# Splitting weight conversion and weight-block preparation into two streams in a fused attention and two-layer feed-forward kernel

## The chip, the cores and the metric

The kernel runs on one core of one Trainium2 chip. The metric is the device time of one execution in microseconds (us). Three runs of the kernel before gave 1201.35, 1202.36 and 1206.76 us; their median, 1202.36 us, is what the change is compared with.

## The reference

Attention with RMS-normalised queries and keys, then two feed-forward layers over the same 1792 tokens.

```python
q, k, v: (4 batches, 12 heads, 448 tokens, 64)
attn = softmax(rmsnorm(q, g_q) @ rmsnorm(k, g_k).T / 8)      # with max subtraction
x = (attn @ v), heads joined: (1792, 768)
h = relu(x @ w_in)                     # w_in  768 x 2048
y = (h * h) @ w_out                    # w_out 2048 x 768
g = y @ w_gate;  val = y @ w_val       # 768 x 1536 each
out = (g * sigmoid(g) * val) @ w_out2  # w_out2 1536 x 768, out (1792, 768)
```

## The kernel before

All results are float32. A feed-forward product is computed with each operand cut in a high part (a cast to the multiplier's format) and a low part (what the cast left over), as high by high, high by low and low by high: three matmuls for one. Against that, the blocks are combined in a seven-product scheme (Strassen's), so that a 2 by 2 block of products takes seven groups P1 to P7 instead of eight. The inputs of the groups are sums and differences of blocks of weights (A11, A12, A21, A22) and of activations (B11, B21, B22, T1 to T4).

**Stages.** Attention comes first. Then for each layer (ph is 0 or 1): an up stage, in which a *quad* (two 128-column slabs of the up weights) yields seven groups of 9 matmuls for each of two token halves (tp is 0 or 1), 14 groups in all; and a down stage of 7 x ng steps of 18 matmuls (ng is 8 in the first layer, 6 in the second), in the order P2, P5, P3, P1, P6, P7, P4. The first up stage has 8 quads, the second 12.

**Weights.** They arrive as 64-bit words, 768 KB a slab, in one of two *raw regions* (L245). Four instructions convert a slab to float32 in one of five buffers called conv: a ScalarE cast (L282) and on VectorE one tensor_scalar (L283) and two scalar_tensor_tensor (L256). A *block* is then a high cast on ScalarE (L458) and a low subtraction on VectorE (L259) into one of the five slots of the ring. The even slabs of the down weights are converted straight into the area dn during the down stage (area jobs); the odd ones during the up stage, sent to DRAM (wkeep, L331) and brought back (L339).

**Up results.** Groups are evicted from PSUM (ps) by ScalarE or VectorE into 448-column slots of xacc, taken from a list called free. Each finished block, and the sums T1, T2 and T4 (GpSimd) and T3 (VectorE), is sent to DRAM (hid, L960). A down step n fetches its pair of blocks (448 KB, L1153), casts it (L1166) and subtracts for the low part (L997) into one of three buffers; this splitting is called cleave, and step n does it for step n + 2.

**What sets the order.** Every engine runs its own instructions in the order in which the program issues them. One generator, stream, yields conversions, sums, casts and low parts in a fixed sequence. pump, called once in each step, takes instructions from it until a budget of VectorE time is spent or the next one's gate is closed; need takes them regardless until the block that TensorE wants is there. A raw slab may be converted three counts of clock after its load was issued (the clock counts groups, two for a down step). All DMAs of this part are issued by SyncE's queue (SP), which waits in order too.

## Time and profile before

| | |
|---|---|
| time, median of 3 runs | 1202.36 us |
| the profiled execution's own time | 1212.9 us |
| its span, first to last instruction | 1211.1 us |
| TensorE (PE) busy | 1151.8 us, 95% |
| VectorE (DVE) busy | 893.8 us, 74% |
| ScalarE (ACT) busy | 627.6 us, 52% |
| GpSimd (POOL) busy | 328.7 us, 27% |
| chain that ended last | PE 69%, DVE 13%, DMA 7%, ACT 6% |
| DMA moved | 183.30 MB, mean 151 GB/s |

The profiled execution took 10.5 us more than the median run. A PE that is called busy need not be at its peak: the granted clock fell in parts of the span, and a matmul takes longer there. The shares are averages over attention (to about 251.7 us), the first up stage (to 472.2 us), the first down stage (to 719 us), the second up stage (to 1031.5 us) and the second down stage; the rows further down are by stage.

### The profile page before, as it was taken

How to read it: one execution, taken by the hardware profiler on the slowest of the kernel's cores; microseconds unless marked ns; L12 is line 12 of the kernel's file. 1: busy time of each engine (PE TensorE's matmuls, PEld its weight loads, DVE VectorE, ACT ScalarE, POOL GpSimd, SP SyncE). 2: the span in 40 equal slices, each digit the busy share in tenths (PEclk: the TensorE clock that was granted, in tenths of full speed). 3: DMA queues.
4: the chain of work that ended last, by engine and by line, in shares of the span. 5: the costliest groups of instructions: out<-in, count | busy, mean ns of one | idle time of the engine just before them, and what ended most of it. 6: DMA issues, size and time to landing. Idle time of an engine off the chain costs nothing.

```text
span 1211.1 us, 17115 instructions
## 1 busy us (share of the span) xinstructions
PE 1151.8 (95%) x6164; PEld 960.0 (79%) x6164; DVE 893.8 (74%) x1185; ACT 627.6 (52%) x1031; POOL 328.7 (27%) x304
## 2 busy tenths in 40 slices
PE   8999999999998998778999999999999999789998
PEld 5555555579887886667999999999999999678997
DVE  7777888678887887567766787868678595776553
ACT  6777886668454555343544445444343433445332
POOL 5899999621422334000000000202112020200000
PEclk9999999999999998888999999999999999899999
DMA  6444331114766768943543400635244453944554
GB/s 172 113 117 127 94 100 56 40 33 134 268 233 206 225 210 303 322 147 113 167 144 122 122 31 25 209 126 193 98 152 141 136 198 106 332 144 122 167 168 136
DMA packets 112997, 183.30 MB, mean 151 GB/s; under 512 B 13329, under 2 KB 94993, under 8 KB 112913
## 3 DMA queue, kind: packets, MB, share of 16 engines
q1 hardware_dynamic: 112592, 182.22, 46.6%
q8 instruction: 48, 0.79, 0.3%
q14 instruction: 37, 0.30, 0.1%
q10 hardware_dynamic: 320, 0.00, 0.0%
HBM read 125.96 MB, written 56.05 MB: 150 GB/s over the span
## 4 chain that ended last, share of the span: by engine, by line
PE 69%; DVE 13%; DMA 7%; ACT 6%; issue 4%; SPq 1%; POOL 1%; ACTq 0%; DVEq 0%; POOLq 0%
PE ps L1035 29%; PE ps L1200 23%; PE s L707 5%; PE s L692 5%; DMA xacc<-in_moe_w_in_dram 2%; DVE conv L256 2%; ACT xacc L1000 2%; PE s L663 2%; DVE xacc L997 2%; DVE ring L259 2%; PE s L631 2%; PE s L728 2%; DMA dn<-hid 1%; DMA xacc<-in_moe_w_out_dram 1%; DVE conv L283 1%
## 5 line engine op out<-in xcount | busy, mean ns | idle before, releaser
L997 POOL TENSOR_TENSOR xacc<-xacc 128x448 f32<-128x448 f32 x84 | 116.2, 1406 | 648.4 <-DVE xacc L997 503.7
L1200 PE MATMUL ps<-xat,ring 128*128 128x448 f32 x1008 | 222.4, 383 | 24.6 <-ACT ring L458 12.7
L1200 PEld LDWEIGHTS ps<-xat,ring 128*128 128x128 f32 x1008 | 197.8, 197 | 49.3 <-ACT ring L458 14.9
L1035 PE MATMUL ps<-xb,ring 128*128 128x448 f32 x1080 | 228.7, 367 | 0.9 <-ACT xacc L1000 0.9
L1035 PEld LDWEIGHTS ps<-xb,ring 128*128 128x128 f32 x1080 | 202.7, 188 | 20.5 <-ACT xacc L1000 1.3
L1200 PE MATMUL ps<-xab,ring 128*128 128x448 f32 x756 | 162.6, 376 | 13.4 <-ACT ring L458 5.9
L1200 PEld LDWEIGHTS ps<-xab,ring 128*128 128x128 f32 x756 | 144.6, 193 | 31.2 <-ACT ring L458 7.3
L1035 PE MATMUL ps<-xat,ring 128*128 128x448 f32 x720 | 159.3, 370 | 5.3 <-DVE xacc L997 5.3
L1035 PEld LDWEIGHTS ps<-xat,ring 128*128 128x128 f32 x720 | 135.9, 189 | 19.6 <-DVE xacc L997 6.8
L259 DVE TENSOR_TENSOR ring<-conv,ring 128x384 fp32r<-128x384 f32 x118 | 83.8, 725 | 61.1 <-ACT ring L458 60.0
L1035 PE MATMUL ps<-xab,ring 128*128 128x448 f32 x540 | 119.4, 371 | 3.9 <-ACT ring L458 3.9
L1000 ACT ACTIVATE xacc<-ps 128x448 f32<-128x448 f32 x148 | 77.9, 547 | 78.6 <-PE ps L1035 62.5
L997 DVE TENSOR_TENSOR xacc<-ps,xacc 128x448 f32<-128x448 f32 x180 | 106.5, 615 | 15.6 <-PE ps L1035 9.7
L1035 PEld LDWEIGHTS ps<-xab,ring 128*128 128x128 f32 x540 | 102.3, 190 | 15.0 <-ACT ring L458 4.3
L256 DVE SCALAR_TENSOR_TENSOR conv<-xacc,conv 128x768 int32<-128x768 int32 x108 | 111.3, 1031 | 3.4
L666 DVE TENSOR_REDUCE mxz<-s 112x2 f32<-112x896 f32 x96 | 100.4, 1088 | 16.5 <-PE s L663 16.3
L458 ACT CAST ring<-dn 128x384 fp32r<-128x384 f32 x82 | 41.7, 514 | 135.0 <-PE ps L1200 103.4
L698 POOL TENSOR_TENSOR sg<-p 112x896 f32<-112x896 f32 x46 | 96.9, 2107 | 14.2 <-ACT p L694 14.2
L458 ACT CAST ring<-conv 128x384 fp32r<-128x384 f32 x118 | 58.5, 510 | 79.4 <-DVE conv L256 34.0
L694 ACT ACTIVATE p<-s 112x896 f32<-112x896 f32 x96 | 87.8, 919 | 20.2 <-PE s L692 15.3
L1000 ACT ACTIVATE xacc<-xacc 128x448 f32<-128x448 f32 x132 | 74.6, 575 | 45.3 <-DVE xacc L997 43.5
L259 DVE TENSOR_TENSOR ring<-dn,ring 128x384 fp32r<-128x384 f32 x82 | 45.9, 566 | 54.7 <-ACT ring L458 54.5
(97 smaller groups left out, 1459.1 us busy)
## 6 DMA issues: line engine op xcount, KB each, us to landing
hid<-xacc SPq DMA_DIRECT2D x196, 224.0 KB
dn<-hid SPq DMA_DIRECT2D x98, 448.0 KB
xacc<-in_moe_w_out_dram SPq DMA_DIRECT2D x28, 768.0 KB
xacc<-in_moe_w_in_dram SPq DMA_DIRECT2D x16, 768.0 KB
xacc<-in_moe_w_gate_dram SPq DMA_DIRECT2D x12, 768.0 KB
xacc<-in_moe_w_val_dram SPq DMA_DIRECT2D x12, 768.0 KB
raw<-in_k_dram SPq DMA_DIRECT2D x24, 224.0 KB
raw<-in_q_dram SPq DMA_DIRECT2D x24, 224.0 KB
```

What stands on the lines that cost most here:

```text
L256: nc.vector.scalar_tensor_tensor(out=out, in0=in0, scalar=scalar, in1=out, op0=op, op1=ALU.bitwise_or)
L259: nc.vector.tensor_tensor(out=out, in0=a, in1=b, op=ALU.subtract)
L458: fn(*args)
L666: nc.vector.tensor_reduce(out=mxz[:, c, 0:P:D], in_=ps[:CP, :, :S], op=ALU.max, axis=AX.X)
L692: nc.tensor.matmul(ps[:CP, a, :S], lhs, rhs, start=(w == 0), stop=(w == 3))
L694: nc.scalar.activation(out=p, in_=ps[:CP, :, :S], func=AF.Exp)
L698: nc.gpsimd.tensor_tensor(out=sg, in0=p_t[pi, 2 * w], in1=p_t[pi, 2 * w + 1], op=ALU.add)
L707: nc.tensor.matmul(ps[s, :S], v_t[pi][:, a, c * D:(c + 1) * D], p[:, a, :], start=(c == 0), stop=(c == NCH - 1),)
L997: eng.tensor_tensor(out=o, in0=a, in1=b, op=op)
L1000: nc.scalar.activation(out=slot(s), in_=src, func=func)
L1035: nc.tensor.matmul(ps, w[:, wi, kk * P:(kk + 1) * P], xk[:, xi, kk * S:(kk + 1) * S], start=bool(first and mm == 0), stop=(mm == 3 * KT - ...
L1200: nc.tensor.matmul(ps_of(ps[tp, o]), w[:, wi, o * P:(o + 1) * P], h[:, hi, tp * S:(tp + 1) * S], start=bool(first and m == 0), stop=(g == ...
```

## The change

The one stream becomes two. convert_all (queue C) converts slabs in their order as soon as a slab has landed and a conv buffer is free; stream (queue B) makes sums and blocks, and waits by gates for what C has made. The low subtraction of a block is put in a third list (L), and is issued at the earliest in the call of pump after the one that issued its cast. pump goes through L, B, C in this order. Buffers are given back by name (spent, busy) instead of by position.

```diff
+    def convert_all():
+        for n, (ph, what, a, b, i) in enumerate(jobs):
+            if what == "area":
+                yield from area_job(ph, a, i)
...
+            c = convs[k % NCONV]
+            free_ = lambda k=k: k < NCONV or k - NCONV in spent
...
+                yield from convert(i, c, free_)
...
-    def block(entry, src, also=None):
+    def block(entry, src, key, gate=None, since=None, done=None):
         n = at[entry]
         r = ring[n % RING]
+        def low():
+            minus(r[:, 1], src, r[:, 0].bitcast(F32))
+            ready.add(n)
...
         yield act(nc.scalar.copy, r[:, 0], src,
-                  gate=lambda: state["used"] >= n - RING + 1 and (also is None or also()))
-        yield dve(0.55, minus, r[:, 1], src, r[:, 0].bitcast(F32))
-        ready.add(n)
+                  gate=lambda: state["used"] >= n - RING + 1 and (gate is None or gate()),
+                  soft=lambda: state["tick"] > (since() if t is None else t))
+        lows.append((state["tick"], n, low))
...
+    def emit(limit, spend, streams):
+        state["tick"] += 1
+        while True:
+            for s in streams:
+                if s == "L":
+                    if lows and lows[0][0] < state["tick"] and limit():
+                        lows.pop(0)[2]()
+                        spend(0.55)
+                        break
+                    continue
+                op = peek(s)
+                if can(op) and (op[0] == "act" or limit()):
+                    cost = run_op(s)
...
     def pump(budget):
-        state["debt"] = min(state["debt"] + budget, budget + 1.5)
+        state["debt"] = min(state["debt"] + budget, budget + 2.0)
...
+        emit(lambda: state["debt"] > 0, spend, "LBC")
```

A third raw region is laid over xacc slots 3 to 6 when these are free. It is claimed in the first up stage from quad 2 on (and again early in a down stage), and the free list has four slots fewer while it is. A load takes the region that was emptied first, and in the up stages a region is filled again three counts of clock after its conversion instead of two.

```diff
     def raw_of(i):
-        a = 16 * S + (b // 2) * 4 * S + (b % 2) * 2 * KH
+        a = (16, 20, 3)[region[i]] * S
...
+        lag = 3 if dn.get("ph") is None else 2
...
+            fit = [r for r in range(3) if valid(r) and (r not in last_in or old(r) + lag <= clock["n"])]
+            region[i] = r = min(fit, key=old)
```

The sums T1 to T4 are issued one count after their inputs instead of up to three, and a slot goes back to the free list when its last reader has been issued (drop). In the down stage the fetch of step n + 5 becomes that of step n + 4, a block from wkeep may be cast two counts after its bring instead of three, pump is called twice in a step with half the budget, and the low half of a cleave goes behind the second call. The first fetches of a down stage are issued in the P3 groups instead of after P7.

```diff
-            for new, needs in (("T1", {"B11": 3, "B12": 1}), ("T3", {"B22": 1, "T1": 1}), ("T2", {"B22": 2, "T1": 3}),
-                               ("T4", {"B21": 3, "T2": 3})):
+            for new, needs in (("T1", ("B11", "B12")), ("T3", ("B22", "T1")), ("T2", ("B22", "T1")), ("T4", ("B21", "T2"))):
...
-                    t = when[new] = max(when[x] + d for x, d in needs.items())
+                    t = when[new] = max(when[x] for x in needs) + 1
...
-                    bring(ph, 1)
-                    stage(ph, 0)
-                    bring(ph, 2)
-                    stage(ph, 1)
-                    bring(ph, 4)
-                    stage(ph, 2)
+                if q_ == last and p == "P3":
+                    bring(ph, 1 + 3 * tp)
+                    stage(ph, tp)
+                    bring(ph, 2 + 3 * tp)
+                    stage(ph, 1 + tp)
...
+                rate = 2.8 if n < 2 * ng else 2.3
+                pump(rate / 2)
                 cleave(n + 2, 0)
-                cleave(n + 2, 1)
                 run_due()
-                stage(ph, n + 5)
+                stage(ph, n + 4)
...
-                pump(2.9 if n < 2 * ng else 2.2)
+                pump(rate / 2)
+                cleave(n + 2, 1)
```

No engine has an instruction more or less than before; what changes is the order, and which buffer is used. Three places show it. The lines of the changed kernel have other numbers: L289, L261, L264 and L267 are what L283, L256, L259 and L262 were, L1014, L351, L360, L247 and L1217 what L960, L331, L339, L245 and L1153 were, and L1054 is L997.

The first place is DVE in the first up stage, around the end of one quad and the beginning of the next; rows with conv on both sides of an int32 operation are conversions, rows that write ring are low parts. Before:

```order
L259 TENSOR_TENSOR ring_85<-conv_77,ring_85 128x384
L283 TENSOR_SCALAR conv_79<-conv_79 128x768
L256 SCALAR_TENSOR_TENSOR conv_79<-xacc,conv_79 128x768 x2
L283 TENSOR_SCALAR conv_80<-conv_80 128x768
L256 SCALAR_TENSOR_TENSOR conv_80<-xacc,conv_80 128x768 x2
L997 TENSOR_TENSOR xacc<-ps,xacc 128x448
L283 TENSOR_SCALAR conv_76<-conv_76 128x768
L256 SCALAR_TENSOR_TENSOR conv_76<-xacc,conv_76 128x768 x2
L259 TENSOR_TENSOR ring_82<-conv_78,ring_82 128x384
```

Now:

```order
L264 TENSOR_TENSOR ring_85<-conv_76,ring_85 128x384
L289 TENSOR_SCALAR conv_76<-conv_76 128x768
L261 SCALAR_TENSOR_TENSOR conv_76<-xacc,conv_76 128x768 x2
L267 TENSOR_TENSOR ssum<-conv_76 128x384
L264 TENSOR_TENSOR conv_76<-conv_80,conv_76 128x384
L1054 TENSOR_TENSOR xacc<-ps,xacc 128x448
L264 TENSOR_TENSOR ring_82<-conv_77,ring_82 128x384
L264 TENSOR_TENSOR ring_86<-conv_80,ring_86 128x384
L289 TENSOR_SCALAR conv_77<-conv_77 128x768
L261 SCALAR_TENSOR_TENSOR conv_77<-xacc,conv_77 128x768 x2
```

The three conversions that stood together ahead of a block's low part are spread between low parts and sums.

The second place is SP at the end of the first up stage, where the results of the last quad are sent and the first pieces of the down stage (dn) are fetched. Before:

```order
L960 DMA hid<-xacc 128x448
L331 DMA wkeep<-conv_80 128x768
L245 DMA xacc<-in_moe_w_out_dram 128x1536
L960 DMA hid<-xacc 128x448 x3
L339 DMA dn<-wkeep 128x2x384
L1153 DMA dn<-hid 128x896
L339 DMA dn<-wkeep 128x2x384
L1153 DMA dn<-hid 128x896
L339 DMA dn<-wkeep 128x2x384 x2
L1153 DMA dn<-hid 128x896
```

Now:

```order
L351 DMA wkeep<-conv_79 128x768
L247 DMA xacc<-in_moe_w_out_dram 128x1536
L1014 DMA hid<-xacc 128x448 x15
L360 DMA dn<-wkeep 128x2x384
L1217 DMA dn<-hid 128x896
L360 DMA dn<-wkeep 128x2x384
L1217 DMA dn<-hid 128x896
L1014 DMA hid<-xacc 128x448
L360 DMA dn<-wkeep 128x2x384 x3
L1217 DMA dn<-hid 128x896
```

The last raw load and the last wkeep now stand fifteen sends ahead of the first fetch instead of three, and five wkeep pieces are fetched here instead of four.

The third place is DVE at the first two steps of the first down stage. Rows that write xat are low halves of a cleave, rows that write dn from xacc or dn convert an area slab. Before, from the cleaves of steps 1 and 2 on:

```order
L997 TENSOR_TENSOR xat<-dn,xat 128x896 x2
L997 TENSOR_TENSOR xacc<-xacc 128x448
L283 TENSOR_SCALAR dn<-dn 128x2x384
L256 SCALAR_TENSOR_TENSOR dn<-xacc,dn 128x2x384 x2
L259 TENSOR_TENSOR ring_84<-dn,ring_84 128x384
L283 TENSOR_SCALAR dn<-dn 128x2x384
L256 SCALAR_TENSOR_TENSOR dn<-xacc,dn 128x2x384
```

Now, from the low parts of the first two blocks on:

```order
L264 TENSOR_TENSOR ring_83<-dn,ring_83 128x384
L264 TENSOR_TENSOR ring_84<-dn,ring_84 128x384
L1054 TENSOR_TENSOR xat<-dn,xat 128x896
L264 TENSOR_TENSOR ring_85<-dn,ring_85 128x384
L264 TENSOR_TENSOR ring_86<-dn,ring_86 128x384
L264 TENSOR_TENSOR ring_82<-dn,ring_82 128x384
L289 TENSOR_SCALAR dn<-dn 128x2x384
L261 SCALAR_TENSOR_TENSOR dn<-xacc,dn 128x2x384 x2
L1054 TENSOR_TENSOR xacc<-xacc 128x448
L289 TENSOR_SCALAR dn<-dn 128x2x384
L261 SCALAR_TENSOR_TENSOR dn<-xacc,dn 128x2x384
L1054 TENSOR_TENSOR xat<-dn,xat 128x896
```

The blocks of the first five steps come ahead of the first conversion instead of the first block alone, and the cleave of step 2 comes behind one and a half conversions.

## Rows read from the trace of the kernel before

**Rows 1.** Windows: us; busy us and instructions of each engine; clock, DMA share, GB/s.

```profile
251.70:472.20 220.50, 210.34 (x1012) 191.11 (x1008) 183.27 (x233) 129.24 (x239) 64.40 (x47) 0.98 0.60 198
472.20:567.40 95.20, 70.59 (x289) 60.23 (x288) 59.02 (x83) 37.20 (x57) 7.31 (x6) 0.87 0.66 232
567.40:719.00 151.60, 151.60 (x720) 137.66 (x721) 110.88 (x143) 69.04 (x102) 0.00 (x0) 0.98 0.39 120
719.00:1031.50 312.50, 312.50 (x1514) 283.85 (x1513) 234.32 (x343) 133.23 (x238) 44.91 (x33) 1.00 0.41 136
1031.50:1110.70 79.20, 65.84 (x291) 56.88 (x289) 56.62 (x80) 33.95 (x54) 5.99 (x4) 0.94 0.57 197
1110.70:1207.50 96.80, 96.78 (x467) 87.58 (x467) 51.53 (x71) 36.04 (x55) 0.00 (x0) 1.00 0.50 158
```

**Rows 2.** Timeline, PE, first up stage: start, us, instruction, count, idle time before.

```profile
255.44 3.81 PE L1035 MATMUL ps<-xb,ring 128*128 128x448 f32 x18
259.09 3.81 PE L1035 MATMUL ps<-xat,ring 128*128 128x448 f32 x18
```

**Rows 3.** Timeline, one late slab in the first up stage, four engines.

```profile
375.40 0.76 SPq L245 DMA_DIRECT2D xacc<-in_moe_w_in_dram  x1
...
381.85 0.89 ACT L282 ACTIVATE conv<-xacc 128x768 f32<-128x768 f32 x1 [10.14 <-DMA xacc<-in_moe_w_in_dram]
...
382.77 0.56 DVE L283 TENSOR_SCALAR conv<-conv 128x768 int32<-128x768 int32 x1 [4.82 <-ACT conv L282]
...
385.91 3.73 PE L1035 MATMUL ps<-xab,ring 128*128 128x448 f32 x9 [3.90 <-ACT ring L458]
```

**Rows 4.** Timeline, from the first up stage to the first down stage.

```profile
468.45 0.59 SPq L339 DMA_DIRECT2D dn<-wkeep  x1
469.10 0.66 SPq L1153 DMA_DIRECT2D dn<-hid  x1
...
470.22 1.98 PE L1035 MATMUL ps<-xlast,ring 128*128 128x448 f32 x9
...
476.31 0.94 ACT L1166 CAST xat<-dn 128x896 fp32r<-128x896 f32 x1 [2.73 <-DMA dn<-hid]
...
477.72 0.74 PE L1200 MATMUL ps<-xat,ring 128*128 128x448 f32 x1 [5.51 <-ACT ring L458]
```

**Rows 5.** Timeline, from the second up stage to the second down stage.

```profile
1024.88 0.59 SPq L1153 DMA_DIRECT2D dn<-hid  x1
...
1027.96 0.77 SPq L1153 DMA_DIRECT2D dn<-hid  x1
...
1029.31 0.94 ACT L1166 CAST xab<-dn 128x896 fp32r<-128x896 f32 x1 [11.90 <-DMA dn<-hid]
...
1036.54 0.94 ACT L1166 CAST xab<-dn 128x896 fp32r<-128x896 f32 x1 [2.22 <-DMA dn<-hid]
```

**Rows 6.** Groups by line, DVE, 465 to 570 us: busy us, mean ns, idle before.

```profile
L997 DVE TENSOR_TENSOR xat<-dn,xat 128x896 fp32r<-128x896 f32 x18 | 19.8, 1100 | 21.6 <-ACT xat L1166 21.6
L256 DVE SCALAR_TENSOR_TENSOR dn<-xacc,dn 128x768 int32<-128x768 int32 x16 | 15.3, 957 | 0.5
L259 DVE TENSOR_TENSOR ring<-dn,ring 128x384 fp32r<-128x384 f32 x12 | 6.5, 552 | 2.0 <-ACT ring L458 2.0
...
L283 DVE TENSOR_SCALAR dn<-dn 128x768 int32<-128x768 int32 x8 | 4.4, 555 | 7.0 <-ACT dn L282 7.0
```

**Rows 7.** Timeline, DVE and POOL side by side, second down stage's first steps.

```profile
1029.53 7.97 POOL L997 TENSOR_TENSOR xacc<-xacc 128x448 f32<-128x448 f32 x5 [0.71 <-DVE xacc L997]
...
1031.56 1.48 DVE L259 TENSOR_TENSOR ring<-dn,ring 128x384 fp32r<-128x384 f32 x1
```

**Rows 8.** Windows, first down stage's first 30 us; the last figure is GB/s.

```profile
472.20:483.90 11.70, 5.78 (x19) 4.42 (x19) 5.70 (x8) 6.30 (x11) 7.31 (x6) 0.71 1.05 402
483.90:502.00 18.10, 13.63 (x56) 11.59 (x56) 12.47 (x17) 6.55 (x9) 0.00 (x0) 0.91 1.01 350
```

**Rows 9.** Chain of waits in order of time, near 304 us: start, us, what.

```profile
303.86 5.10 DMA hid<-xacc
```

More of the change, by code (lines that the diff above doesn't have):

```diff
@@ L69 @@
     clock = {"n": 0}
-    state = {"turn": 1, "used": 0, "debt": 0.0, "down": -1, "step": -1, "limit": 4}
+    state = {"turn": 1, "used": 0, "debt": 0.0, "down": -1, "step": -1, "limit": 4, "tick": 0, "third": False}
     def slot(s):
@@ L247, in load_raws, with waiting, dve, act @@
             nsent["n"] += 1
[L249 to L253 removed]
+    def waiting(rs):
+        return [i for i in sent if i not in turned and region[i] in rs]
+    def dve(cost, fn, *args, gate=None, soft=None):
+        return ("dve", cost, fn, args, gate, soft)
+    def act(fn, *args, gate=None, soft=None):
+        return ("act", 0.0, fn, args, gate, soft)
     def stt(out, in0, scalar, op):
@@ L441, in stream @@
-                if n % 3 != 2 and evens < ng:
-                    assert p == "P2" or evens > g
-                    evens += 1
-                    yield from conv_next(ph, "area", None)
-                if ph == 0 and p == "P1" and g % 2:
-                    yield from conv_next(1, "quad", carry)
-    steps = stream()
-    ahead = []
-    def peek():
-        if not ahead:
-            ahead.append(next(steps, None))
-        return ahead[0]
-    def run_op():
-        _, cost, fn, args, _ = ahead.pop()
+                    t, tk = spare.pop(0)
@@ L1133, in up @@
                         state["down"] = 100 * ph + level
+                if ph == 0 and q_ >= 2 and not state["third"] and len(free) >= 8 and all(s in free for s in (3, 4, 5, 6)):
+                    claim_third()
                 if q_ == last and tp == 1 and p == "P7":
@@ L1192, in down @@
                 if n == ng - 1:
+                    assert not due
                     free.clear()
+                if n < ng and not state["third"] and all(s in free for s in (3, 4, 5, 6)):
+                    claim_third()
+                if n == 2 * ng:
+                    state["third"] = False
+                if n == 3 * ng - 1:
+                    assert not waiting((2,))
                 first = g == 0 and p in ("P2", "P5", "P1")
```

321 lines of the change are left out of this document (175 added, 146 removed).

## The prediction

> **What bounds the kernel now.** I read the page first: TensorE is busy 95% of the span, so a time can only come out of the places where it isn't, or where its clock is low. The busy time by windows finds them [rows 1]. In the second up stage and in the late parts of both down stages PE has no idle time. In the other three windows it has, and its granted clock is 0.98, 0.87 and 0.94 there. The price of a stage without any loss comes from two neighbouring pieces of the timeline: 18 matmuls start 3.65 us after the 18 before them [rows 2], so a down step is 3.65 us, a group of nine 1.825. In the second half 467 matmuls take 96.8 us [rows 1], 3.73 us a step. From that the losses:
>
> First up stage: 8 quads of 14 groups are 112 groups, 204.4 us; it takes 220.5: 16.1 us lost. First down stage: the 720 matmuls of the third window leave 288 of 1008, 16 steps, 58.4 us; they take 95.2 (the gap ahead of them included): 36.8 lost. Second down stage: 756 - 467 = 289 matmuls, 16 steps, 59.9 us; they take 79.2: 19.3 lost. Together 72 us, and that is all that a new order of the same instructions can win.
>
> Then who ends PE's waits. In the up stage, once in most quads, a slab that is late: its load goes out at 375.40, ScalarE stands 10.14 us until it lands at 381.85, DVE converts from 382.77, and PE, which had waited 3.90 us, goes on at 385.91 at a lower clock [rows 3]. At the end of that stage SP issues the first fetch of the down stage at 468.45, the activations follow at 469.10 and are cast at 476.31, and PE has waited 5.51 us [rows 4]. In the down stage DVE is short of nothing but order: the low halves of 18 cleaves had 21.6 us of idle time ahead of them, spent waiting for the high casts, and the conversions 7.0 [rows 6]. DVE is busy only 59.0 of 95.2 us there [rows 1], while PE waits for it.
>
> **The change, part by part.** No engine gets or loses an instruction. What is won is waiting, and each stage has a new limit that decides how much.
>
> First down stage. P7 of the last quad ends three groups ahead of the last group's start, at 470.22 - 5.5 = 464.7 [rows 4]. Before, SP reaches the first fetch 3.7 us after that, because a late wkeep and a raw load stand just ahead of it; now fifteen sends lie between. With nothing in its way the fetch goes out at about 465, the activations 0.65 us behind it. In the second down stage, where SP is free, they need 1029.31 - 1024.88 = 4.4 us [rows 5], so they are there at 470.1, cast and subtracted (0.94 and 1.10 us) at 472.1, as PE finishes its last group. The 5.5 us go.
>
> Late next is step 2. Its fetch is the eighth of this burst instead of the seventh. The seventh was cast 1036.54 - 1024.88 = 11.7 us after the first [rows 5]; one more wkeep piece is 0.39 MB, 1.0 us at 402 GB/s [rows 8]. So it lands at 465.5 + 12.7 = 478.2, the fifth wkeep piece a microsecond earlier. DVE's piece of step 0 in the new order is three low parts, one sum, one and a half conversions and the cleave: 3 x 0.552 + 0.6 + 2 x 0.555 + 3 x 0.957 + 1.1 = 7.3 us [rows 6], from 477.1 to 484.4. Beside it POOL makes the last quad's sums. A low part that took 0.552 us took 1.48 beside those, five of which fill 7.97 us [rows 7]. The low parts here stand ahead of most of POOL's work, so I take two to three such lengthenings, 2.4 us; the bounds are none and, if all eight of its two-input instructions suffer, 7.4. Step 2 starts at 486.8 instead of 479.4.
>
> This is where a page speaks against the change. The Trainium skill ("SBUF — State Buffer", section "Who interferes with whom") says that a VectorE instruction with two SBUF inputs and a GpSimd instruction that reads SBUF exclude each other, the later one standing still for the whole of the other. By it DVE would lose up to the full 8 us of POOL's sums, 5.6 more in each down stage, and the forecast would be 11 us higher; the 0.93 us of the row is less than a POOL sum of 1.6, so the trace bears out the conflict and not the whole price.
>
> From there DVE sets the pace. In the new order steps 0 to 15 hold 16 cleave lows, 18 scalar_tensor_tensor, 9 tensor_scalar, 19 ring lows, 26 sums of that size and one 0.6: 17.6 + 17.2 + 5.0 + 24.8 + 0.6 = 65.2 us [rows 6] against 58.4 for PE. What is left after step 0, 57.9 us, ends at 544.7, when step 17 can start; with 3 us for gaps and slabs that land late, 548. Without loss it would start at 472.1 + 17 x 3.65 = 534.2. The loss is 14, with a microsecond for the clock 15 instead of 36.8: 22 us won. DMA hides behind this: by step 7 the new order has asked for about 14.4 MB since 465 (8 wkeep pieces of 0.39 MB, 9 fetches of 0.46, 5 raw slabs of 0.79, 14 sends of 0.23), 35.8 us at 402 GB/s or 41.1 at 350 [rows 8], so until 501 or 506, and DVE comes to the last of these slabs at about 510. If that cover is gone, the second rival below is the price. Bounds of this term: 10 (every step waits for DMA) to 29.
>
> Second down stage. It had no late SP, so its first step starts at 1031.5 as before. Step 2's activations come one wkeep piece later, 1037.5; DVE's first piece ends at 1036.4 + 7.3 + 2.4 = 1046.1, 7 us late. Steps 0 to 11 hold 12 x 1.1 + 12 x 0.957 + 6 x 0.555 + 38 x 0.552 + 0.6 = 49.6 us; the remaining 42.3 end at 1088.4, with 2 us for gaps 1090.4, and step 13 without loss would be at 1080.0. The loss is 10.4 instead of 19.3: 9 us won, bounds 3 and 14.
>
> First up stage. Raw loads go to three regions, and a slab is converted about a quad ahead of its use instead of three to five groups ahead, so the wait of rows 3 falls on engines and not on PE. But DVE needs 183.3 of 204.4 us [rows 1], and the new order puts the conversions of the whole stage into its first five sixths, where it leaves DVE nothing over. I take 7 us of loss instead of 16.1: 9 won. The row nearest is the busy time of DVE; bounds are 13 (only the first quads' tightness remains) and minus 4 (below nothing, by the waits of the third rival).
>
> The second up stage and attention have no loss to give; their orders shift by an instruction or two, and I cost them at nothing, since PE covers both (234 us of DVE in 312.5).
>
> Sum: 22 + 9 + 9 = 40 us. The profiled execution took 1212.9, so 1172.9; the median was 10.5 lower, which makes 1162.
>
> **Rivals.** *DMA takes the place of DVE.* A fetch is now issued two steps, 7.3 us, ahead of its cast, one step later than before. One at the head of the queue needs 4.4 us, one behind six others 8.6 [rows 5]. While raw slabs are loaded each may be 1.3 us late: 8 + 6 steps of P2 give 18 us back, and 40 - 18 = 22 leave 1180. For it: 402 and 350 GB/s right there [rows 8]. Against: a fetch that is late hits ScalarE first, and the cast has a further step in hand. The Trainium skill ("DMA: Bandwidth & Descriptors", "Where 436 GB/s comes from") gives some 358 GB/s as what HBM grants a core; 14.4 MB would then take 40.2 us, and this rival would be likelier; the 402 of the trace speak against so low a ceiling.
>
> *Slower: slots that are still being sent.* The third region takes four slots, so the free list holds six instead of ten in the up stage, and in each quad from the fourth on the evictions of P5 (both halves) and of P6's first go into slots whose send was issued one or two groups, 1.8 to 3.7 us, before. A send can take 5.10 us [rows 9]. Three waits of 3.3 are 9.9 us a quad; ScalarE is busy 129.2 us in 8 quads, 16.2 of 25.5, and has 9.4 to spare: so it decides from sends of about 5 us on. At 8.6 us, as long as a fetch in the burst, the waits are 20.4 and exceed it by 11 us in each of five quads: 55 lost, 31 won in the down stages, 24 slower, 1226. Against it: sums are issued earlier, SP's queue isn't tied to PE's steps, and DMA is busy only 0.60 of that stage.
>
> *No change.* The streams wait for each other through the five conv buffers and the same ring, the third region is rarely free, and what the low parts win is lost in the new bursts: 1200.
>
> **How the numbers follow.** The forecast has 0.61 (its own range 1146 to 1175), the DMA rival 0.24 (1175 to 1194), no change 0.06, slower 0.09. About 0.5%, 6 us, is what can be told from no change. Faster by more: 0.85; within: 0.06; slower: 0.09. The range that leaves out two in ten runs from 1142, the sum of the best bounds being 56 won and so 1146, less a little for the clock, to 1190.
>
> **What would show it.** Right, if PE's gap ahead of the first down stage is under 1.5 us, the first 16 steps there take 70 to 77 us instead of 95.2 with DVE busy over 85% of them, a gap of several us stands ahead of step 2 in both down stages, no low half of a cleave waits long for its cast, and the first up stage takes 208 to 215 us. Wrong, if ScalarE waits in the down stage mostly for DMA (first rival), if evictions in the up stage wait for hid sends and PE's gaps there grow (second), or if the second up stage, now without a gap, gets some.

## The result and the profile after

The changed kernel takes 1175.4 us (median of 4 runs, 1174.2 to 1177.2) where the kernel before takes 1203.9 (4 runs, 1201.4 to 1206.8): a ratio of 0.976, 95% interval 0.974 to 0.979. That is 28.5 us faster; 40 were forecast. The time lies inside the outer range of 1142 to 1190, and just beyond the forecast's own 1146 to 1175, on the border to the 1175 to 1194 of the DMA rival: the number alone does not decide between the two, the stages below do. The profiled execution took 1177.2 us, 35.7 less than the profiled one of before.

The windows of the changed kernel, cut at the same points of the program as [rows 1]: us; busy us and instructions of each engine; clock, DMA share, GB/s.

```profile
251.46:467.74 216.28, 211.31 (x1012) 191.17 (x1008) 182.08 (x236) 135.45 (x245) 69.83 (x49) 0.98 0.65 217
467.74:543.23 75.49, 64.83 (x288) 57.27 (x288) 64.84 (x94) 35.31 (x55) 4.76 (x4) 0.93 0.74 260
543.23:692.79 149.56, 147.16 (x720) 135.03 (x721) 103.78 (x132) 66.48 (x98) 0.00 (x0) 1.00 0.38 117
692.79:1006.56 313.77, 312.75 (x1514) 283.55 (x1512) 232.84 (x342) 133.50 (x240) 44.88 (x33) 1.00 0.41 136
1006.56:1076.10 69.54, 63.46 (x290) 56.40 (x290) 57.49 (x82) 33.12 (x54) 4.76 (x3) 0.95 0.64 222
1076.10:1171.80 95.70, 95.20 (x469) 87.57 (x467) 50.38 (x68) 36.15 (x56) 0.00 (x0) 1.00 0.50 160
```

Stage by stage against [rows 1]: first up stage 220.5 to 216.3, first 16 steps of the first down stage 95.2 to 75.5, the rest of it 151.6 to 149.6, second up stage 312.5 to 313.8, first 16 steps of the second down stage 79.2 to 69.5, the rest 96.8 to 95.7. Sum of the differences: 35.4 us, of which 29.4 in the two starts of down stages. (L1092 and L1271 are the matmuls that were L1035 and L1200, L490 and L1230 the casts of blocks and activations that were L458 and L1166; L1293 evicts.)

The step into the first down stage, PE and then DVE, which answer to [rows 4] and [rows 7]: start, us, instruction, count, idle time before and its releaser.

```profile
465.71 2.02 PE L1092 MATMUL ps<-xlast,ring 128*128 128x448 f32 x9
467.74 0.47 PE L1271 MATMUL ps<-xat,ring 128*128 128x448 f32 x1
468.75 0.47 PE L1271 MATMUL ps<-xat,ring 128*128 128x448 f32 x1 [0.54 <-DVE xat L1054]
471.63 9.01 PE L1271 MATMUL ps<-xat,ring 128*128 128x448 f32 x35 [2.41 <-DVE ring L264]
...
467.32 1.38 DVE L1054 TENSOR_TENSOR xat<-dn,xat 128x896 fp32r<-128x896 f32 x1 [0.21 <-ACT xat L1230]
468.62 1.55 DVE L1054 TENSOR_TENSOR xacc<-xacc 128x448 f32<-128x448 f32 x1
470.10 0.61 DVE L1054 TENSOR_TENSOR xacc<-ps,xacc 128x448 f32<-128x448 f32 x1
470.63 2.36 DVE L264 TENSOR_TENSOR ring<-dn,ring 128x384 fp32r<-128x384 f32 x2
```

The 5.5 us ahead of the stage are gone. What stands there now is 2.41 us at the third matmul, which waits for the low part of the first weight block (L264); DVE has a sum and an eviction ahead of it. Beside POOL's sums the times that these instructions take alone, 1.09, 0.62 and two of 0.55 us, have become 1.38, 1.55 and 2.36 (the two together): 2.5 us more in all, and the prediction had taken 2.4.

Next the queue of SyncE (SPq) and ScalarE a few steps on.

```profile
474.02 0.32 SPq L1217 DMA_DIRECT2D dn<-hid  x1
474.39 5.31 SPq L1014 DMA_DIRECT2D hid<-xacc  x6
480.89 0.32 SPq L1217 DMA_DIRECT2D dn<-hid  x1
481.26 0.52 SPq L360 DMA_DIRECT2D dn<-wkeep  x1
...
476.76 0.95 ACT L1230 CAST xat<-dn 128x896 fp32r<-128x896 f32 x1 [0.65 <-PE ps L1271]
485.43 0.51 ACT L490 CAST ring<-dn 128x384 fp32r<-128x384 f32 x1 [7.72 <-DMA dn<-wkeep]
485.84 0.94 ACT L1230 CAST xat<-dn 128x896 fp32r<-128x896 f32 x1
491.68 0.51 ACT L490 CAST ring<-dn 128x384 fp32r<-128x384 f32 x1 [4.90 <-DMA dn<-wkeep]
```

The fetch at 480.89 fills a staging buffer that DVE has only just emptied, and the wkeep piece stands behind it in the queue: asked for at 481.26, cast at 485.43, after ScalarE has stood for 7.72 us. PE's gaps of 1.74 and 2.76 us at 493.9 and 497.1 come behind the second of these late casts.

### The profile page after: what moved, and what is told of

It reads as the page before. It is cut to its first block, busy times and chain, and to the rows that moved or that the text cites. A ratio compares the mean times of both kernels' runs of the same rounds, so it can differ in the third digit from the quotient of the medians.

```text
span 1175.4 us, 17088 instructions
## 1 busy us (share of the span) xinstructions
PE 1138.8 (97%) x6164; PEld 954.2 (81%) x6164; DVE 890.7 (76%) x1185; ACT 629.0 (54%) x1031; POOL 330.4 (28%) x304
## 4 chain that ended last, share of the span: by engine, by line
PE 50%; DVE 3%; DMA 1%; issue 1%; ACT 1%; SPq 0%; DVEq 0%; ACTq 0%
PE ps L1271 26%; PE ps L1092 24%; DMA dn<-wkeep 1%; DMA xacc<-in_moe_w_out_dram 1%; DVE xacc L1054 1%; DVE conv L261 0%; DVE dn L261 0%; DVE ring L264 0%; DVE conv L289 0%; ACT xat L1230 0%; DVE xab L1054 0%; DVE xat L1054 0%; SPq L360 0%; ACT dn L288 0%; DVE dn L289 0%
## 5 line engine op out<-in xcount | busy, mean ns | idle before, releaser
L1054 POOL TENSOR_TENSOR xacc<-xacc 128x448 f32<-128x448 f32 x84 | 117.1, 1407 | 623.3 <-DVE xacc L1054 411.6
L1092 PE MATMUL ps<-xb,ring 128*128 128x448 f32 x1080 | 231.1, 369 | 1.0 <-DVE ring L264 1.0
L1271 PE MATMUL ps<-xat,ring 128*128 128x448 f32 x1008 | 212.2, 372 | 13.1 <-DVE xat L1054 5.5
L1092 PEld LDWEIGHTS ps<-xb,ring 128*128 128x128 f32 x1080 | 203.8, 189 | 22.1 <-DVE ring L264 1.4
L1271 PEld LDWEIGHTS ps<-xat,ring 128*128 128x128 f32 x1008 | 192.1, 191 | 33.1 <-DVE xat L1054 7.2
L1271 PE MATMUL ps<-xab,ring 128*128 128x448 f32 x756 | 158.7, 372 | 6.5 <-DVE xab L1054 3.6
L1092 PE MATMUL ps<-xat,ring 128*128 128x448 f32 x720 | 159.9, 370 | 5.0 <-DVE ring L264 5.0
L1271 PEld LDWEIGHTS ps<-xab,ring 128*128 128x128 f32 x756 | 144.0, 191 | 21.0 <-DVE xab L1054 5.6
L1092 PEld LDWEIGHTS ps<-xat,ring 128*128 128x128 f32 x720 | 136.0, 189 | 19.1 <-DVE ring L264 5.3
L1054 DVE TENSOR_TENSOR xacc<-ps,xacc 128x448 f32<-128x448 f32 x180 | 108.3, 617 | 46.8 <-PE ps L1092 38.8
L490 ACT CAST ring<-dn 128x384 fp32r<-128x384 f32 x80 | 41.0, 514 | 161.4 <-PE ps L1271 122.8
L264 DVE TENSOR_TENSOR ring<-conv,ring 128x384 fp32r<-128x384 f32 x127 | 90.0, 719 | 38.5 <-ACT ring L490 38.2
L1092 PE MATMUL ps<-xab,ring 128*128 128x448 f32 x540 | 118.3, 368 | 0.0
L261 DVE SCALAR_TENSOR_TENSOR conv<-xacc,conv 128x768 int32<-128x768 int32 x108 | 110.4, 1022 | 2.5
L1092 PEld LDWEIGHTS ps<-xab,ring 128*128 128x128 f32 x540 | 101.3, 188 | 10.9 <-issue 0.7
L490 ACT CAST ring<-conv 128x384 fp32r<-128x384 f32 x127 | 62.8, 508 | 85.0 <-PE ps L1092 30.8
L752 POOL TENSOR_TENSOR sg<-p 112x896 f32<-112x896 f32 x46 | 96.8, 2104 | 15.6 <-ACT p L748 15.6
L264 DVE TENSOR_TENSOR ring<-dn,ring 128x384 fp32r<-128x384 f32 x80 | 46.6, 588 | 63.3 <-ACT ring L490 63.1
```

The source lines that it names most:

```text
L261: nc.vector.scalar_tensor_tensor(out=out, in0=in0, scalar=scalar, in1=out, op0=op, op1=ALU.bitwise_or)
L264: nc.vector.tensor_tensor(out=out, in0=a, in1=b, op=ALU.subtract)
L490: fn(*args)
L752: nc.gpsimd.tensor_tensor(out=sg, in0=p_t[pi, 2 * w], in1=p_t[pi, 2 * w + 1], op=ALU.add)
L1054: eng.tensor_tensor(out=o, in0=a, in1=b, op=op)
L1092: nc.tensor.matmul(ps, w[:, wi, kk * P:(kk + 1) * P], xk[:, xi, kk * S:(kk + 1) * S], start=bool(first and mm == 0), stop=(mm == 3 * KT - ...
```

## The experiments

Stage times are of one profiled execution each; times in all are medians of 4 runs (of one for the second profile of the kernel before), with the kernel before run beside them on the same chip (its medians there were 1200.4 to 1205.7 us). Executions of one kernel differ by up to 15 us (1197.2 to 1212.2 for the kernel before); its second profile says in what for the most part, and so it comes first. (The 73.8 us in some expectations leave out the gap of 1.67 us ahead of the 17th step, which the windows here and in [rows 1] count with the first 16: with it, 75.5.)

**The kernel before, profiled a second time.**

> The kernel before, unchanged, for a second profile of it. The profiled execution on which the prediction's sums rest took 1212.9 us where the median of the runs is 1203.9, and the profiled execution of the changed kernel 1177.2 against a median of 1175.4. Theory one: the 9 us belong to the stages that the change works on, an execution with more loss than usual there. Then this one takes 1201 to 1207 us, and its first down stage has lost 28 to 32 us in its first 16 steps instead of 36.8, or its first up stage 8 to 12 instead of 16.1. Theory two: the profile itself costs the 9 us, or they lie in stages without a loss. Then the first 16 down steps take 93 to 97 us again, and the up stage 219 to 222.

It took 1200.8 us, a span of 1199.0 instead of 1211.1. Its first 16 down steps and its second up stage, windows as above:

```profile
474.30:565.45 91.15, 67.23 (x290) 57.78 (x289) 58.40 (x83) 35.85 (x54) 5.47 (x5) 0.90 0.67 237
...
714.50:1020.90 306.40, 306.40 (x1513) 284.01 (x1512) 233.39 (x343) 132.55 (x238) 45.01 (x33) 1.00 0.41 139
```

The second up stage has no gap in either execution and a granted clock of 1.00 (the 2.4 GHz level) in both, and took 306.4 us here and 312.5 in [rows 1]. One group of 18 matmuls, here and in the first profile:

```profile
787.45 3.81 PE L1035 MATMUL ps<-xab,ring 128*128 128x448 f32 x18
791.09 1.18 PE L1035 MATMUL ps<-xat,ring 128*128 128x448 f32 x5
```

```profile
793.47 3.88 PE L1035 MATMUL ps<-xab,ring 128*128 128x448 f32 x18
797.19 0.99 PE L1035 MATMUL ps<-xat,ring 128*128 128x448 f32 x4
```

It is 3.64 us to the next group, or 3.72: by the start times of all matmuls 202.7 or 206.7 ns each, on average over a group, and hardly anything else where PE has no gap and the clock is full. Of the 4,284 matmuls from the first up stage on some 2,934 had the slower pace in the first profile and 243 in the second. Take 4 ns for each of them from the spans and 1199.4 and 1198.0 are left. So theory two is right in the main: the excess lies in stages without a loss, and it is not what profiling costs, since this profiled execution is as fast as the other runs. Both of its ranges were missed all the same: the first 16 down steps took 91.2 us, 4.0 less than in the first profile, and the first up stage 222.5, 2.0 more. Below, "at equal pace" is a span less 4 ns for each such matmul: arithmetic on one execution, not a time of the chip.

**The changed kernel, profiled a second time.**

> The changed kernel, unchanged, for a second profile of it. In the traces so far a matmul starts 202.7 or 206.7 ns after the one before it, at a granted clock of 1.00 in both, and a stretch keeps its pace for as long as PE has no gap; the first profile of the changed kernel had 2,664 of its up and down matmuls at 206.7, the second of the kernel before 243. Theory (the two paces are most of what differs between executions of one kernel, and the profile's excess over the median that the prediction took off): span minus 4 ns for each matmul at the slower pace comes to 1162 to 1167 us again (1164.7 in the first profile), whatever the span is, and the loss in the first 16 steps of both down stages is the same within 1.5 us. Rival (the executions differ in their waits): that difference leaves 1168 or more, or 1161 or less.

Median 1170.7 us; span 1171.1 with 1,107 matmuls at the slower pace, at equal pace 1166.7 (1164.7 in the first profile, which had 2,664). First 16 steps 75.6 and 69.7. Theory confirmed: at equal pace the change wins 1198.7 - 1165.7 = 33 us.

**Without the third region.**

```diff
-                if ph == 0 and q_ >= 2 and not state["third"] and len(free) >= 8 and all(s in free for s in (3, 4, 5, 6)):
+                if False and ph == 0 and q_ >= 2 and not state["third"] and len(free) >= 8 and all(s in free for s in (3, 4, 5, 6)):
...
-                if n < ng and not state["third"] and all(s in free for s in (3, 4, 5, 6)):
+                if False and n < ng and not state["third"] and all(s in free for s in (3, 4, 5, 6)):
```

> The changed kernel with two regions for raw slabs instead of three; the rest of the change stays. Theory one (the order of the low halves makes the gain of the down stages): first down stage's first 16 steps stay at 72 to 77 us (73.8 with the third region), second's at 69 to 72; the first up stage gets back most of its wait, 216.3 becomes 219 to 222. In all 1178 to 1183 us. Rival (the raw slabs that the third region lets in earlier make the gain): the first 16 steps of the first down stage go to 84 us or more, and the time to 1190 to 1200.

1183.9 us (1178.8 to 1188.8); first 16 steps 78.0 and 71.9; first up stage 217.2 with two more gaps (1.36 and 2.16 us); at equal pace 1175.3. The time, the first down stage's 16 steps and the up stage each lie 1 to 2 us outside what theory one named, and far from the rival. The third region is worth some 10 us, of which 2.5 in either start of a down stage and 4 (at equal pace) in the first up stage: it helps, and is not what made the down stages' gain.

**Low halves right behind their casts.**

```diff
-        lows.append((state["tick"], n, low))
+        yield dve(0.55, low)
```

> The changed kernel in which the low half of each weight block follows in VectorE's order right behind its cast, as in the kernel before, instead of a call later; two streams, third region and fetches stay. Theory one (the order of the low halves makes the gain of the down stages): VectorE waits for the casts again, 10 us or more of idle time in the first 16 steps of the first down stage, which take 83 to 92 us instead of 73.8; second down stage 74 to 79 instead of 69.5; the time 1190 to 1200. Rival (the raw slabs let in earlier make the gain): 1176 to 1181, the first 16 steps at 77 or less.

1195.1 us, 0.990 of the kernel before; at equal pace 1191.2, so 25 us of the 33 go with this one line. First 16 steps 82.7 and 75.7; another 6 us are lost behind them in each down stage, in gaps of up to 1.7 us, most of them at the ends of groups. Groups by line of DVE, low halves in 467 to 541 us (busy, mean ns, idle before), in this kernel and in the changed one:

```profile
L264 DVE TENSOR_TENSOR ring<-dn,ring 128x384 fp32r<-128x384 f32 x11 | 7.5, 697 | 10.1 <-ACT ring L490 10.1
```

```profile
L264 DVE TENSOR_TENSOR ring<-dn,ring 128x384 fp32r<-128x384 f32 x12 | 7.7, 664 | 1.0 <-ACT ring L490 0.9
```

DVE stands for casts again, which themselves stand for late wkeep pieces. A call later it finds them done, and does conversions in the time between.

**The fetches as before.**

```diff
-                if q_ == last and p == "P3":
-                    bring(ph, 1 + 3 * tp)
-                    stage(ph, tp)
-                    bring(ph, 2 + 3 * tp)
-                    stage(ph, 1 + tp)
+                    bring(ph, 1)
+                    stage(ph, 0)
...
-                pump(rate / 2)
                 cleave(n + 2, 0)
+                cleave(n + 2, 1)
                 run_due()
-                stage(ph, n + 4)
+                stage(ph, n + 5)
...
-                pump(rate / 2)
-                cleave(n + 2, 1)
+                pump(rate)
```

> The changed kernel with the fetches of up results as in the kernel before: first burst at P7 of the last quad, then one step earlier than in the change, both halves of a cleave ahead of the pump. Streams and third region stay. Theory one (the fetches give only the gap ahead of the first down stage, the order of the low halves the rest): first matmul of the first down stage waits at most 1 to 2 us, since it is the blocked queue and not the place of the fetch that made it late; first 16 steps 74 to 79 us; the time 1174 to 1182. Rival (the later fetch is what lets the low halves and conversions run in VectorE's gaps, because a cleave no longer stands ahead of them): first 16 steps 82 us or more in the first down stage, 75 or more in the second, the time 1186 to 1195.

The first burst stands behind P7 of the last quad again; the end of the up stage and each later step do both halves of the cleave ahead of the pump and fetch one step further ahead, and a step pumps once, at its end.

1175.6 us, no different from the change. But theory one failed at its gap: PE waits 6.38 us ahead of the first down stage and 5.06 ahead of the second. The first 16 steps took 80.2 and 72.4 us, the first between the ranges of theory and rival, the second below the rival's. The fetch was not late: SP asked for the first activations at 461.24 us, in the changed kernel at 460.97. ScalarE, then PE:

```profile
464.29 0.51 ACT L490 CAST ring<-dn 128x384 fp32r<-128x384 f32 x1
467.99 0.51 ACT L490 CAST ring<-dn 128x384 fp32r<-128x384 f32 x1 [3.19 <-DMA dn<-wkeep]
470.11 0.51 ACT L490 CAST ring<-dn 128x384 fp32r<-128x384 f32 x1 [1.62 <-DMA dn<-wkeep]
471.48 0.51 ACT L490 CAST ring<-dn 128x384 fp32r<-128x384 f32 x1 [0.85 <-DMA dn<-wkeep]
...
473.41 0.93 ACT L1230 CAST xat<-dn 128x896 fp32r<-128x896 f32 x1
...
474.39 0.74 PE L1271 MATMUL ps<-xat,ring 128*128 128x448 f32 x1 [6.38 <-ACT xat L1230]
```

Four casts of weight blocks stand ahead of the first cast of activations in ScalarE's order, and three of them wait for a piece on its way, 5.66 us in all. And behind the first 16 steps this kernel is faster than the change, 145.9 us instead of 149.6. So its two halves had to be parted.

**Only the later fetches as before.** The first burst stays as in the change; the rest of the edit is the one above.

> The changed kernel with its own first burst, but the fetch and the two halves of the cleave of every later down step placed as in the kernel before (one step earlier, ahead of the pump). Theory (of the change's two moves of the fetches, the earlier first burst wins and the later step loses, and in the run with both undone they cancel): no gap over 1 us ahead of the down stages; first 16 steps 73 to 75 us in the first and 66.5 to 68.5 in the second down stage, the steps behind them 145.5 to 146.5 in the first, without the gap of 1.7 us at the end of a group (149.6 and 75.7, 69.5 in the changed kernel); the time 1160 to 1168, and span minus 4 ns for each matmul at the slower pace 1156 to 1160. Rival (the place of the step's fetch does nothing; mix was faster by its other two edits): 149 to 150 behind the first 16 steps, 75 to 77 in them, the time 1170 or more.

1164.6 us; first 16 steps 69.6 and 67.9, the first figure better than the 73 to 75 expected. Behind them 148.7 without a gap, outside the 145.5 to 146.5 that were expected: all 720 matmuls had the slower pace, 720 x 206.7 ns = 148.8. At equal pace 1155.4. So the earlier first burst wins 14 us (1169.4 with both undone) and the new order of the later steps loses 10 (1165.7 with both in place). That order is three moves, of fetch, cleave and pump; this run does not say which of them costs what. One place of the loss in the changed kernel, ScalarE and PE at the end of a group:

```profile
541.40 0.51 ACT L490 CAST ring<-dn 128x384 fp32r<-128x384 f32 x1 [2.29 <-PE ps L1271]
541.82 0.93 ACT L1230 CAST xat<-dn 128x896 fp32r<-128x896 f32 x1
542.66 1.83 ACT L1293 COPY xacc<-ps 128x448 f32<-128x448 f32 x4
...
543.23 5.13 PE L1271 MATMUL ps<-xat,ring 128*128 128x448 f32 x24 [1.67 <-ACT xacc L1293]
```

Half a pump ahead of the evictions that free PE's banks puts a block cast there which waits 2.29 us for PE itself; behind it and the cast of a cleave they start at 542.66, 1.5 us after the group's last matmul began. In this run the block cast at the same place belongs to the pump of the step before and waits for DVE, the evictions start at 535.05, 0.6 us before the group's last matmul begins, and the gap is gone. A pump that stands behind is not enough for that: the kernel before has 4.18 us at this place, where the block cast waits 2.87 us for DVE.

**wkeep asked for first.**

```diff
                 cleave(n + 2, 0)
+                bring(ph, n + 6)
                 run_due()
                 stage(ph, n + 4)
...
-                bring(ph, n + 5)
```

> The changed kernel with one thing moved: in a down step the slab that comes back from DRAM (wkeep) is asked for ahead of the sends and of the fetch of the up result, one step earlier, not behind them. In the changed kernel SyncE stands 5 to 8 us at such a fetch, until VectorE has freed its staging buffer, and ScalarE then waits 7.7, 4.9 and 1.9 us for wkeep pieces that were issued behind it. Theory (that queue is what is left of the loss): ScalarE's wait for wkeep in the first 16 steps of the first down stage falls from 16.3 us to under 6, PE's gaps around matmul 90 (1.7 and 2.8 us) go, the steps take 70 to 72 us instead of 75.7, the second down stage gains 1 to 3; the time 1168 to 1173. Rival (DMA is full there and every piece is late anyway): the wait stays over 12 us, the steps at 74 to 77.

1166.7 us; first 16 steps 69.1 and 66.2, better than expected. Waits of ScalarE in the first 16 steps, in the changed kernel and in this one:

```profile
ACT ring L490 <- DMA dn<-wkeep: 16.3, 6, 7.7
```

```profile
ACT ring L490 <- DMA dn<-wkeep: 4.9, 6, 1.6
```

DMA moved 285 GB/s in these steps instead of 260. The pieces were late because they were asked for late, not because the transfers were slow. ScalarE's wait is no measure of the loss by itself, though: in the run above it waits 13.0 us for such pieces, and its first 16 steps take 69.6.

**The first low half earlier.**

```diff
                 cleave(tp, 1)
+                if tp == 0:
+                    need(at[ph, "P2", -1])
```

> The changed kernel with the low half of the first down block put two instructions earlier in VectorE's order, ahead of a sum that stands beside POOL's sums and of the last eviction. Theory (VectorE's order makes the 2.4 us gap at the third matmul of each down stage): the gap falls under 0.8 us in both stages, the first 16 steps take 73.5 to 74.5 us instead of 75.7 and 67.5 to 68.5 instead of 69.5; in all 3 us, 1170 to 1174. Rival (the sum and the eviction only move behind and are missed a step later): gaps of the same size appear within the next two steps and nothing is won.

1176.0 us, no gain; 76.0 us. The gap at the third matmul fell to 0.94, and this came two steps later:

```profile
479.22 3.33 PE L1273 MATMUL ps<-xat,ring 128*128 128x448 f32 x9 [2.96 <-DVE xat L1054]
```

The rival is right: what one instruction gains ahead of two others is missed two steps later.

**The sums of POOL on DVE.**

```diff
-            tt(eng, slot(m[name]), slot(m[a]), slot(m[b]), ALU.subtract)
+            tt(nc.vector, slot(m[name]), slot(m[a]), slot(m[b]), ALU.subtract)
```

> The changed kernel with the 84 sums that POOL does in the up stages given to VectorE, in the same places. Theory one (a VectorE instruction that reads two SBUF operands and a POOL sum hold each other up): in the changed kernel's trace the VectorE instructions that lie beside POOL's sums are 59.7 us longer than the same forms alone, 0.71 us for each sum, and VectorE takes 0.62 us for such a sum itself. Then its busy time stays as it is, within 15 us, no two-input form is lengthened any more, the up stages take the same time within 3 us, and the time is 1170 to 1179. Rival (POOL relieves VectorE): VectorE gets 52 us more, the first up stage, where it is busy 90%, takes 225 us or more, and the time is 1185 to 1200.

1174.5 us, no difference. Groups of DVE over the span, in the changed kernel and in this one:

```profile
L1054 DVE TENSOR_TENSOR xacc<-ps,xacc 128x448 f32<-128x448 f32 x180 | 108.3, 617 | 46.8 <-PE ps L1092 38.8 <-ACT xacc L1057 7.9
...
L264 DVE TENSOR_TENSOR ring<-conv,ring 128x384 fp32r<-128x384 f32 x127 | 90.0, 719 | 38.5 <-ACT ring L490 38.2
```

```profile
L1054 DVE TENSOR_TENSOR xacc<-ps,xacc 128x448 f32<-128x448 f32 x180 | 108.5, 619 | 50.1 <-PE ps L1092 42.9 <-ACT xacc L1057 6.9
...
L1054 DVE TENSOR_TENSOR xacc<-xacc 128x448 f32<-128x448 f32 x148 | 87.1, 619 | 1.5 <-ACT xacc L1057 0.7
L264 DVE TENSOR_TENSOR ring<-conv,ring 128x384 fp32r<-128x384 f32 x127 | 68.7, 552 | 37.3 <-ACT ring L490 37.2
```

The form of the low parts, which reads two operands from SBUF, loses its lengthening (719 to 552 ns); the one that reads PSUM had none (617, 619). DVE does 84 sums more and is busy 882.9 us instead of 890.7: POOL had taken nothing off it.

**Three edits at once: first burst of the change, later fetches as before, wkeep first and the first low half early.**

> The changed kernel's first burst with the fetch of every later step, and both halves of its cleave, placed as in the kernel before; wkeep asked for ahead of sends and fetch, and the first low half early, as in the two single edits. Theory (the old place of the fetch was as good as the new one, its one loss being the gap ahead of each down stage): no gap over 1 us ahead of the down stages, first 16 steps 69 to 73 and 66 to 69 us, the time 1164 to 1172. Rival (the new place is the better one and the old fetch only looked equal because the runs differ): first 16 steps 75 or more in the first down stage, the time 1174 to 1180.

1159.3 us (1155.3 to 1166.9), ratio to before 0.965 (0.958 to 0.972); first 16 steps 67.0 and 67.4; at equal pace 1153.3. It beats both kernels, and the 1164 to 1172 expected.

**That kernel with the sums on DVE.**

> The best kernel so far with the 84 sums of the up stages on VectorE instead of POOL. By the run of the same edit on the changed kernel (VectorE's busy time 882.9 us instead of 890.7, times equal) it should make no difference of more than 3 us: 1156 to 1163. Rival: the sums of the last quad lie on VectorE just where the down stage starts, and now that nothing else is late there the first 16 steps of each down stage get 3 to 5 us longer: 1163 to 1170.

1153.3 us (1150.6 to 1159.7), ratio 0.960 (0.954 to 0.965), at equal pace 1150.1: the lowest time of all and under the 1156 to 1163 expected, though its interval overlaps that of the kernel without this edit, so that a gain of the edit is not shown. First 16 steps 66.4 and 68.8; the rival's 3 to 5 us did not come.

**That kernel (sums on POOL) with raw slabs loaded as soon as a region is free.**

```diff
-                if not types:
-                    state["limit"] = len(loads) if ph else limits[1]
+                state["limit"] = len(loads) if ph and not types else max(state["limit"], limits[1])
```

> The best kernel so far (first burst as in the change, later fetches as before, wkeep asked for first, first low half early) with one rule less: in the first up stage the fifth and later raw slabs may be loaded as soon as their region is free, not only when all operand kinds have been prepared. In all kernels of the changed order PE waits 5 us at about 313 us; the slab for the third quad is asked for at 287.6 to 289.2 there, converted from 293 on, and VectorE has no gap from 296 to 314. Theory (that wait comes from the late load): slabs asked for 5 us earlier or more, the gap of 5 us falls to under 2, the first up stage takes 207 to 211 us instead of 213.2; 1153 to 1157 in all. Rival (VectorE's sum of work up to there decides, not the load): the gap stays over 4 us.

1161.7 us; the first up stage 216.2 instead of 213.2. The slabs were asked for 32.3 us into the stage instead of 35.9, since SP had to wait for DVE to leave the region (17.1 us for the first slab, 3.4 for the second): 3.6 earlier, not 5. The gap split into 1.60, 1.16 and 6.68 us, the last at 323 us. That speaks for the rival (DVE's work up to there; in the changed kernel DVE is busy 17.9 of the 18.0 us from 296 to 314), but a load 10 us earlier wasn't tried; the 5 us gap stays open.

## Why the prediction came out as it did

**The terms.** First down stage: 22 forecast, 19.7 measured between the first profiles (15.6 from the second profile of the kernel before), 75.5 us inside the 70 to 77 that were named, DVE busy 64.8 of 75.5 (86%). Second: 9 forecast, 9.7 measured. That the first came so close is in part luck: up to step 2 less was lost than forecast and behind it more, for a reason that the sum did not have (below). Nor was DVE's work the limit yet: with nearly the same work in another order (64.6 and 62.3 us of DVE) two of the kernels above do the 16 steps in 69.1 and 67.0. First up stage: 9 forecast, 4.2 measured, and the stage's 216 us lie just outside the 208 to 215 named. But some 980 of its 1,008 matmuls had the slower pace, 3.9 us, against some 250 of before, 1.0 us: at equal pace 7 us. What is left there is one gap of 4.96 us at 313 us with seven matmuls at a low clock behind it (2.98 us). Attention and the second up stage gave nothing, as forecast, though a gap of 1.0 us came into the latter, which the prediction had named as a sign against it. The late parts of the down stages, put at nothing, gave 2.0 and 1.1. Sum 35.4 of 40.

**The step that failed: from the profile to the median.** "The profiled execution took 1212.9, so 1172.9; the median was 10.5 lower, which makes 1162." The 10.5 us were taken off as if every run of the changed kernel would be faster by as much. They were that execution's pace: 2,934 matmuls by 4 ns is 11.7 us. The changed kernel's first profile has 2,664 of them too, 10.7 us, and its other runs lie within 3.0 us of it, so they probably had them as well; they were not profiled. With all matmuls at the faster pace it stands at 1164.7. The [rows 2] showed 3.65 us for 18 matmuls and the second half of [rows 1] 3.73; the prediction wrote both down, used each in its stage, and did not ask what the difference was.

**Step 0 and step 2.** A gap of several us ahead of step 2 was forecast, because its activations come behind one wkeep piece more. It is 0.27 us, and 0.55 in the second down stage. The lateness was there, but it fell on step 0 (2.41 us, DVE's order beside POOL, and matmuls at the low clock behind that gap): step 2 had started 13.2 us into the stage, 5.7 later than without loss, where 7.4 were forecast. Of the 17.1 us lost in the 16 steps (75.5 less 58.4) the other 11.4 lie behind that, where the sum had 7.6, and there the cause was another from step 5 on: wkeep behind a blocked fetch, then evictions. "DMA hides behind this" was counted in megabytes; what counted was SP's order. Here a fetch that waits for a buffer held the piece that stood behind it.

**The gap ahead of the first down stage.** It went, as forecast, but the reason was half right. A fetch that leaves in time isn't enough: with the old burst and a free queue the gap was 6.38 us, because four block casts stood ahead of the first activation cast on ScalarE. That old burst, in the new order, made a gap of 5.06 us ahead of the second down stage too, where the kernel before had none.

**The low halves.** "DVE is short of nothing but order" is the step that the runs bear out best: undoing that order alone gives back 25 of 33 us at equal pace. The undone parts add up to more than the whole (25, 10 for the third region, 14 less 10 for the fetches), so they lean on each other; the split into two streams and the earlier sums T1 to T4 were not undone by themselves.

**The rivals.** Of the first one (fetches a step later cost) the sign was right and the place too: in the first 16 steps of the first down stage ScalarE waited longest for DMA, 16.3 us, and the new order of the steps, the later fetch among it, loses 10 us. Its mechanism, full transfers, is not what made ScalarE wait, by the run that asked for wkeep first. The slower case (slots still being sent) shows once: an eviction waits 3.41 us for a send near 309 us, beside the 4.96 us gap, and ScalarE's waits for sends in the whole stage are 4.7 us, far from the 20.4 a quad that it needed. Nor does that send make the gap: in the kernel of the three edits it costs 0.21 us, and PE still waits 5.31. Nothing became slower.

**The page on DVE and POOL.** The Trainium skill ("SBUF — State Buffer", "Who interferes with whom") lets a VectorE instruction with two SBUF inputs and a GpSimd one that reads SBUF hold each other up, and one with at most one SBUF input, outside its two-port modes, go free. The traces agree in kind: instructions beside POOL's 84 sums are some 54 us longer than the same forms alone, 0.65 us a sum, and those that read PSUM are not (616 and 617 ns). The busy times of the run with the sums on DVE make it 0.71 (890.7 against 882.9 less 84 sums of 0.62); the 59.7 us of its expectation are too many for the count in the trace. An instruction with one SBUF input can be held up too: a tensor_scalar conversion of the kernel before that begins 0.4 us into a sum takes 1.50 us instead of 0.56. The twelve of that kind beside sums are 10 us longer than alone in the kernel before and 1 us in the changed one, whose order puts them elsewhere.

The price of one meeting is what is left of the sum. The low part of [rows 7] begins 0.92 us into a sum that lasts until 1032.63, and ends at 1033.04; so its 0.93 us does not speak for a smaller price, as the prediction reads it. By the full price the forecast would have been 11 us higher; in the start of the first down stage it was 2.5 us, because four such instructions fall beside the sums and wait for the rest of one each.

## What to carry to other kernels

When the same instructions only change places, look at each in-order queue for what stands *behind* an instruction that may wait (a block cast behind a slab, a wkeep piece behind a fetch): here that was worth 7 to 25 us a place at equal pace, and megabytes and busy shares did not show it. Undo each half of a change separately: the two halves of the fetches' move were +14 and -10 and together looked like next to nothing. Before a profile's excess over the median is taken off, see from the starts of matmuls in a stage without gaps whether it lies there.

## What the hardware showed that was not expected

At a granted clock of 1.00 a 128x448 matmul starts 202.7 or 206.7 ns after the one before. A stretch without gaps keeps its pace (1,512 matmuls at 206.7 in one execution of the kernel before, at 202.7 in the other), and where it changed, it did so across a gap of PE in all cases seen but one. It can make up to 17 us of such a kernel (4,284 matmuls by 4 ns), and it makes most of the 12 us between two profiles of the same program. What sets it stays open: no experiment here was made to turn it.

DMA moved 401 GB/s over 7 us at the start of the first down stage, as in [rows 8], above the 358 or so that the Trainium skill ("DMA: Bandwidth & Descriptors", "Where 436 GB/s comes from") gives as a core's share of HBM; here one core ran alone. And 84 sums given to GpSimd cost VectorE 0.65 to 0.71 us each, where it does one itself in 0.62.
